# Inverse roots of four group norms at once: GpSimd's power function in place of Newton steps on VectorE

## The chip, the cores and the metric

The kernel runs on one core of one Trainium2 chip. The core has five engines that run side by side, each with an instruction queue of its own that it works through in order: TensorE (PE in the profile; its weight loads are PEld), VectorE (DVE), ScalarE (ACT), GpSimd (POOL) and SyncE (SP), which here only issues DMAs. An instruction that needs another engine's result waits on a semaphore, and everything behind it in its queue waits too. The metric is the device time of one execution in microseconds (us), lower is better.

## The reference

A residual block of a diffusion network on two images of 512 channels and 64 x 64 pixels: group norm with four groups, SiLU, a 3 x 3 convolution, an embedding added per channel, again group norm, SiLU and convolution, and the input added at the end.

```python
def gn(z, gamma, beta):
    zr = z.reshape(B, G, (C // G) * H * W)          # G = 4, eps = 1e-5
    mu = zr.mean(-1).reshape(B, G, 1)
    var = ((zr - mu) ** 2).mean(-1).reshape(B, G, 1)
    zn = ((zr - mu) / jnp.sqrt(var + eps)).reshape(B, C, H, W)
    return zn * gamma.reshape(1, C, 1, 1) + beta.reshape(1, C, 1, 1)
h = conv3(_silu(gn(x, g1, be1)), w1)
emb = _silu(t_emb) @ w_emb
h = h + emb.reshape(B, C, 1, 1)
h = conv3(_silu(gn(h, g2, be2)), w2)
return x + h
```

A group is 128 channels, so it is one channel tile: 128 partitions, one channel each.

## The kernel before

**Tiling.** The work is cut into eight chunks, numbered 0 to 7: layer, then image, then upper or lower half of the image. Each chunk has four channel tiles as input and four as output. For an input tile the kernel loads the half image (`load_a`), applies group norm and SiLU in one ScalarE instruction with a scale and a bias per partition (`silu`, an ACTIVATE of 128x2112 at L371), and turns the rows into planes for a convolution by transform: ScalarE or VectorE makes a scaled copy (the `k` copies, 128x2145), and VectorE adds and subtracts planes (`rows_a`, `rows_b`; L348). For an output tile, `unit` runs the matmuls of all planes (L401), ScalarE evicts PSUM with scales (L371), and VectorE adds the pieces together (names ending in S, A, s, d, y; L348). In the first layer the result goes to `h_scr` in DRAM; in the second it is accumulated by DMA onto the input that has been copied to the output before. The weights are transformed too (`prep_w1`, `nest_w1`, and `prep_w2` with ScalarE copies of 128x384 and VectorE additions of 128x768).

**Group norm.** `gn_chain` (L452) turns sums per partition into the scale S and the bias B that `silu` uses. A matmul with -1/128 averages over the partitions and spreads the result, VectorE copies it out of PSUM (L469), forms the square of the mean minus the mean of squares (L474 and L475, the negative variance), takes the inverse root, and computes S (L492) and B (L497, L498). It comes in two sizes. For the first layer's first image it runs four times with one group each (n = 1, before 31 us); there the inverse root is a GpSimd instruction, a power with exponent -0.5 (L479). For the other three cases it handles four groups at once (n = 4, 128x4 values):

- `st1`: layer 1, image 1. In the trace VectorE works on it from 105.6 to 111.7 us, in chunk 1; the reader is the SiLU of chunk 2 at 111.71 us.
- `gn2_0`: layer 2, image 0. From 170.1 to 204.4 us, in chunk 2; the reader is the SiLU of chunk 4.
- `gn2_1`: layer 2, image 1. From 275.8 to 319.6 us, in chunks 4 and 5; the reader is the SiLU of chunk 6 at 319.87 us. `gn2` adds two instructions behind the chain (L1078, L1079) for the embedding.

In these three the inverse root is made on VectorE: one step that clamps and halves (L482), a first guess from the bits of the number (L485), and three rounds of Newton's method with three instructions each (L488, L489, L490).

**Order.** The function first lists all operations with their reads and writes (`pl.op`), and then issues them in an order written out by hand: the string `ORDER` (L168) has two characters per operation, its number in base 64. `emit` (L97) walks the string. Each engine thus has a fixed sequence, and the instructions of a chain stand wherever the string puts them: in `st1` and `gn2_1` mostly side by side, in `gn2_0` spread between other VectorE work. GpSimd's queue holds, besides small memsets, the DMAs that accumulate (`sw=True`, L386): pieces of a unit's output onto its rows (`oa`), and from chunk 4 on the results onto the output.

**Names of single operations** that the prediction uses: `u10A`, a 128x1024 addition of VectorE for output tile 0 of chunk 1, which reads two evictions; `u10s`, the next addition there, which reads all four.

Of the kernel before, what the change touches and what calls it, by code (L numbers as in the profile page):

```python
# [11 lines left out]
ALU = mybir.AluOpType  # L12
# [103 lines left out]
def _idx(off, dims):  # L116
# [16 lines left out]
EPS = 1e-5  # L133
# [32 lines left out]


ORDER = (  # L168
    "0R0M000O0N2g0P0T0S0Q0p010U020304050607080o0V1J0n1G0e0m1H0k0t0f0l1I0q0s0r0g0u1L1K1M0v0w0h0x1N0y1O0X1P2Z1Q0z0-250Y"
    "0_2W0i0j1R160Z1a1k3P1S0b1T1l101m190W22121n3X1o2C111U2D1d0a1p2p090A0B0C0D0E0F2F0G0H0I0J0K0L1q132E1r1V141s2G2H1t4t"  # L170
    "1C1u3R2I1W152h2J1v2K1w172L1X2M1x3S181D0d1A1F1B2N3Q1Y1y2O1Z1z1b1-2P4Y1E1c1_1e2s1f4g3U202Q21282S233Y2R2429262T271g"
    "2r2c2U2v2V3T2X1h2d2B2Y0c2a2j2b1i2k2A2y2l1j2z3t2i2m2e2-2o4b2u2q2_2f303n2n313k4a323Z333a3u2t4Z343v3b353c364h2x3738"
    "3d2w393e3C3A3f3m3w3q3B3x453D3g5c3F463h4i3E474d3W5U4k484j493V3i4A4c3G4B4l4C3H3y3K4m4F3p3z3I4G3J6Y3j4H3l4n4I3o4J5W"
    "4f4u4x4K3L4L5X5d4M3r3M51424o3-523_4r4O535V4p544e3s554z564D6Q4-4N574E584s4w6l5B5e5C4q6Z5D5g406m5E415F5Y6n5G5h5H85"
    "5I6S5i5f5p4y435k4v5q865r4P6R5s875u5j5v4Q4T4_5wBK4RBL5x503N4S5y5Z4U5z5-445m4V5l5_5J6T995K625A6a63595n64BM5L3O655o"
    "676c685M5P5a696b5N6d6A5OBO6B666eBa9A6C5t7u6f6V6D5Q6E6o4W6g5R6U6p6h6q8y9B6r6kBN6j6t616u6vBSBPBc6w6xBQ606y6zAD6-6F"
    "73Bb6iBT6G746WBR5b6XAE4X75AF5S76BH786H79777A7B6I6L7C7D7EBeBU7F7J6JBIBW6K7KDI6s6M7LDQBd7cBVBg7M6N6_7d70Bf7N7eBJDR"
    "7G7OBh7f725T7gBY7PBX7Q7hBZ7i7j887k7H7l7m897nDJ7R7o718A7p7S7q7IDT8B7rDS7s7T8DDK8E8F7tDU7v8G8HDM8IEr8JDW8KDY8P7U8Q"
    "DV7V7w8R7WDF7X8S7y8L8U7x8T8V8W8X8z7z8Y8Z8aDGA08b7-8f7Y8g8M808h6O7Z8C7_8iDa8N8j8d818n8kDHDL8-8l8cDO8m8_9C8oDN909D"
    "A1DZDP829E919F8OB49H836P9I9J9K9L929M8e9NDX9O9T847b8p9UEs939VDc9W94Ez9Y8q9Z9a9b978s9c9d9e8r9f989j8t959kEt8u9G9l9P"  # L180
    "9mDbEv8v9QA29nF5Eu9S7a9oB5De9pDdA39qA4AG9hE-96AH9XA59gAI9RD29rA6AJ9i9sALA8AMAKAN8wAO9tAPAQA7AR9xASAX9uATAUAYA99w"
    "AZExE_B6Aa9vEwAcF0AdB8EyD3AeAfABAgAhAiAjAn9yF6AoDfAAAk9zApB9AlAqB78xArBAEbACAsAVBCAtAvBBAuAWBiAwBD9-BjF7AmD4BkBG"
    "AxBlBFBnBoA_BpAyBqAbBrBsD6A-BtBuByD5AzBzB-BwB_B0BvC4BmC5C0D7B1BxC6F9C19_C7EoGWBEC9CACdF1CBCCCeEpCDGOCED8F8CFCgEq"
    "CGC8CJChDACKCLCHCMF3CPCNF2CQCID9F4B3CRFBCiDBCSG8FADgC2GYDhDCGQGXFCCTDiCfC3EcCjDEDjGPDDDlDmDnDoCODpDqDtDrDsGSEdDw"
    "CkCUDxDyClGLDzE2GaDuCmCVE3HuGRCnGeGME4CXCoEeGZE5CYCWCpEfE7G9E8E9CqGNEAEBCrEgECEDEECZEHHhEIEJD_EKD-ENGUDvCaCsEODk"
    "EhB2GcEFEPGTE6EiEQGfHwEjFDGgCtGbEGFEGVCuELEkFFE1GAFGCvE0GdFICwEnFJFKGiFLFMEREMFNI0FOFPFRFTHiHyFUFVFWESI8FbElHvFc"
    "CxGCGhFdETFYFeEmEVFgEWFhEUFiGDFjFSFkFlFHGjFmFnEXFQFqFrI2FsFtHxFwGEFXEYCyGkFxFoGBI1FfFyGlJJFZFpFzI4FuCbGFGmCcCzH-"
    "GnC-HzGoGGGpIAFaI9IGF-GIGrGsJKGtI3GKGuGvGHG-GwGzGxGyFvHjH0JLH1H_H2H3I5H8F_EZH9I6H5KaG_HAG0H4D0HBHlIHG2I7G3HDGJHE"
    "HFEaHGHHC_HmHIHJHKG1HNHnHOG4HPHQIBHTHCHkG5HUGqH7KcHVIIKbHoHRHWD1HpIJIOHMH6HXIPHqNZHLIQHtJMHsIRNYITHSIUIVIWIXIKIY"
    "IZHYIaIeIdIfICIgHcIhHZImIcIDIbInHbHaIMIoIjIEIiIpISILIFHrIrJNIsHdItIuG6IvIwIxIyIkHeI_I-J0JPJ1INIqJ2J5IlIzJQJ6J3JO"  # L190
# [23 lines left out]
    "dQdRdScrexdTd8dqdldrdsdndtdIdudidvdmdVdwdxeydkdzdJdjd-d_d9dUe0e1e2dyc6e3e4dLe8e9dXe5eAeBdKeCeDdYeEeFeHdWdaeIeJeK"
    "dZdbeLeMdceNeOeReSeTeUdeeGeVe7eWeXeYePe6edeeefezegeaf0eheiddeZejgCeQekdff5elf6f7emf8gDf9ecfAe-fBfCf2fEfDebfFfGf1"
    "fHh6e_fIfJeofKfLfPenfMfQfRepfSfTfUesfVereqfWfYfZetfafbfcfdfeffevfXfieufjfkfNewflfgfmfOfnfofpfufhfrfvfwfqfxfyfzf-"
    "fsf_g3gEg1gFgGg4g0gHgIgJg7gKg6g5gLftgNgMgOg8gPgQgRgSgTg2gUgYgVgZg9gagbgAgcgdgWgBgegfghgXgggigjgkglgmgngogrgpgsgq"
    "gtgug_gwh0gxh3h2h1gyh5gzh4g-h7gvh8h9hChAhDhB"
)

@with_exitstack
def kernel(
# [115 lines left out]
    def F(c, n=1, parts=P):  # L338
        return R(fs[0:parts, c:c + n], ("F", np.arange(c, c + n)), n)
# [109 lines left out]
    def small(fn, r, w, name, cost=0.125):  # L449
        pl.op("DVE", cost, fn, regs(*r), regs(*w), name)  # L450

    def gn_chain(layer, b, ct, mes, name, SB=7, slack=2.5, n=1, half=False):  # L452
# [20 lines left out]
        else:  # L473
            small(lambda: V.tensor_mul(out=N.ap, in0=T0.ap, in1=T0.ap), [T0], [N], name)  # L474
            small(lambda: V.tensor_add(out=N.ap, in0=N.ap, in1=T1.ap), [N, T1], [N], name)  # L475
        if n == 1:
            small(lambda: V.tensor_scalar(out=N.ap, in0=N.ap, scalar1=-1.0, scalar2=EPS, op0=ALU.mult, op1=ALU.max),  # L477
                  [N], [N], name)
            pl.op("POOL", 0.85, lambda: nc.gpsimd.tensor_tensor(  # L479
                out=F(rs, n).ap, in0=N.ap, in1=F(NEGH, n).ap, op=ALU.pow), regs(N), regs(F(rs, n)), name)  # L480
        else:
            small(lambda: V.tensor_scalar(out=N.ap, in0=N.ap, scalar1=-EPS, scalar2=0.5, op0=ALU.min, op1=ALU.mult),  # L482
                  [N], [N], name)
            y, u = F(rs, n), F(Fc(n), n)
            small(lambda: V.tensor_scalar(out=y.ap.bitcast(I32), in0=N.ap.bitcast(I32), scalar1=-0.5,  # L485
                  scalar2=float(0x5F3759DF - (2 ** 30 + 2 ** 22)), op0=ALU.mult, op1=ALU.add), [N], [y], name)
            for _ in range(3):
                small(lambda: V.tensor_mul(out=u.ap, in0=y.ap, in1=y.ap), [y], [u], name)  # L488
                small(lambda: V.tensor_mul(out=u.ap, in0=u.ap, in1=N.ap), [u, N], [u], name)  # L489
                small(lambda: V.scalar_tensor_tensor(out=y.ap, in0=u.ap, scalar=1.5, in1=y.ap, op0=ALU.add, op1=ALU.mult),  # L490
                      [u, y], [y], name)
        small(lambda: V.tensor_mul(out=S.ap, in0=F(rs, n).ap, in1=F(g, n).ap), [F(rs, n)], [S], name)  # L492
        if n == 1:
            small(lambda: V.scalar_tensor_tensor(  # L494
# [896 lines left out]
```

## Time and profile before

| what | value |
|---|---|
| three runs | 459.97, 460.64 and 460.56 us; median 460.56 us |
| profiled execution, first to last instruction (span) | 459.7 us; the page gives no other total for it |
| TensorE, VectorE, ScalarE, GpSimd busy | 448.6, 436.9, 401.8, 58.1 us |
| granted TensorE clock, mean | 0.995 |
| GpSimd powers (L437, L479) | 567 ns once; 911, 548, 934 and 933 ns |
| VectorE's Newton instructions (L485, L488 to L490) | 30, 148 to 165 ns each |
| GpSimd's DMA issues (L386) | 41, mean 1207 and 1244 ns; waits before them up to 22.3 us |

How to read it: the span is cut into busy time per engine. A line of the profile names the source line and the engine, what is written and read, its shape and count, and then busy time and mean, or, in a timeline, start, length, and in brackets the idle time just before it and what ended that. Successive instructions of VectorE and ScalarE overlap in the drawing by some 0.08 us, and matmuls by more, so that what an instruction costs in time is the distance from its start to the next start. Two facts of the trace help with orientation: TensorE works with almost no gap, and VectorE and ScalarE are each over 85% busy, so a wait in one place is often only the other side of a wait in another.

### The profile page before, as it was taken

The numbers are of one execution on the slowest core, as the hardware profiler recorded it, in microseconds if no ns is written. First come the engines' busy times: TensorE is split into PE (matmuls) and PEld (weight loads), VectorE is DVE, ScalarE is ACT, GpSimd is POOL, SyncE is SP. The second block draws the span as 40 slices with busy tenths as digits, with TensorE's granted clock in tenths as the row PEclk, the third lists the DMA queues.
The fourth block names the chain that finished last, engine by engine and source line by source line (L and its number), as shares of the span: only waits on it lengthen the run. The fifth ranks groups of instructions, "written<-read, shape, count | busy, mean of one in ns | idle before, by whom it ended". The sixth has DMA issues, their size and how long they took to land. (4 is left out here: it accounts for less than half of the span.)

```text
span 459.7 us, 8124 instructions
## 1 busy us (share of the span) xinstructions
PE 448.6 (98%) x2904; PEld 282.8 (62%) x2904; DVE 436.9 (95%) x811; ACT 401.8 (87%) x611; POOL 58.1 (13%) x82
## 2 busy tenths in 40 slices
PE   8999999999999999999999999999999999999995
PEld 4754334455555566566665666676666666787882
DVE  2899999999999999999999999999899999999995
ACT  5689999999989999999999999868989869757662
POOL 2110010111111101111000001212121223111220
PEclk9899999999999999999999999999999999999999
DMA  8963561587666468577877947798796989676674
GB/s 321 399 210 109 170 192 47 144 255 223 165 177 202 126 188 233 150 237 217 269 223 234 363 163 229 192 224 222 172 244 156 280 221 260 157 186 122 133 141 93
DMA packets 43176, 92.49 MB, mean 201 GB/s; under 512 B 6400, under 2 KB 18048, under 8 KB 43136
## 3 DMA queue, kind: packets, MB, share of 16 engines
q1 hardware_dynamic: 32208, 77.60, 50.1%
q0 software_dynamic: 10640, 14.38, 20.2%
q8 instruction: 22, 0.36, 0.3%
q14 instruction: 18, 0.15, 0.1%
q10 hardware_dynamic: 288, 0.01, 0.0%
HBM read 62.25 MB, written 31.32 MB: 204 GB/s over the span
## 5 line engine op out<-in xcount | busy, mean ns | idle before, releaser
L401 PE MATMUL psum<-ar 128*128 128x256 f16 (+2 forms) x2771 | 427.7, 316 | 3.3 <-ACT ar L371 2.0
L348 DVE TENSOR_TENSOR ar<-ar 128x1024 f16<-128x1024 f16 (+7 forms) x630 | 413.2, 719 | 8.2 <-ACT ar L371 5.4
L401 PEld LDWEIGHTS <-ar 128*128 128x128 f16 (+1 forms) x2763 | 268.6, 98 | 158.9 <-issue 6.9
L371 ACT ACTIVATE ar<-ar 128x512 f16<-128x512 f16 (+6 forms) x186 | 187.1, 1041 | 26.5 <-DVE ar L348 25.0
L371 ACT ACTIVATE ar<-psum 128x512 f16<-128x512 f32 (+3 forms) x250 | 158.8, 680 | 18.8 <-PE psum L401 10.3
L371 ACT ACTIVATE ar<-ar,fs 128x2112 f16<-128x2112 bf16 (+1 forms) x32 | 68.8, 2154 | 3.7 <-DVE fs L494 3.7
L386 POOL DMA_DIRECT2D ar<-ar x26 | 30.8, 1207 | 218.4 <-DVE ar L348 192.1
L386 POOL DMA_DIRECT2D out_dram<-ar x15 | 18.7, 1244 | 55.0 <-DMA ar<-ar 40.1
L371 ACT ACTIVATION_READ_ACCUMULATOR ar<-psum 128x1 f32 x104 | 22.6, 217 | 0.0
L352 DVE TENSOR_SCALAR ar<-ar 128x520 f16<-128x520 f16 (+3 forms) x50 | 19.6, 404 | 0.0
L390 POOL MEMSET ar<- 128x65 f16 (+4 forms) x29 | 5.8, 269 | 95.1 <-DVE ar L348 48.9
L401 PEld LDWEIGHTS <-ones_bf 128*128 128x128 bf16 x88 | 9.1, 109 | 7.0 <-issue 2.1
L401 PE MATMUL psum<-ones_bf 128*128 128x512 bf16 x32 | 8.8, 438 | 1.1 <-DVE ones_bf L405 1.1
L401 PE MATMUL psum<-ar,ones_bf 128*128 128x260 bf16 x56 | 8.0, 296 | 0.0
L371 ACT ACTIVATION_READ_ACCUMULATOR ar<-ar 128x1 f32 x36 | 7.2, 201 | 0.0
L401 PEld LDWEIGHTS psum<-fs,ones_neg 128*128 128x128 f32 x36 | 4.6, 191 | 2.6 <-issue 1.6
L401 PE MATMUL psum<-fs,ones_neg 128*128 128x1 f32 (+3 forms) x36 | 4.5, 243 | 1.5 <-DVE fs L1130 1.3
L1125 DVE BATCH_NORM_STATS2 fs<-ar 128x6 f32<-128x512 bf16 x4 | 2.5, 681 | 3.7 <-DMA ar<-in_x_dram 3.7
L479 POOL TENSOR_TENSOR fs<-fs 128x1 f32<-128x1 f32 x4 | 3.3, 832 | 19.6 <-DVE fs L477 19.5
L438 DVE CAST fs<-gparm 128x16 f32<-128x16 bf16 x1 | 0.2, 175 | 3.0 <-DMA gparm<-in_params_dram 3.0
L439 ACT ACTIVATE s_sb<-tparm 128x18 bf16<-128x18 bf16 x1 | 0.2, 218 | 3.1 <-DMA tparm<-in_t_emb_dram 3.1
L401 PE MATMUL psum<-ar,s_sb 128*2 128x512 bf16 x9 | 2.7, 377 | 0.0
(54 smaller groups left out, 24.4 us busy)
## 6 DMA issues: line engine op xcount, KB each, us to landing
ar<-in_w_dram SPq DMA_DIRECT2D x36, 384.0 KB, 5.1
ar<-in_x_dram SPq DMA_DIRECT2D x16, 552.5 KB, 4.7
h_scr<-ar SPq DMA_DIRECT2D x16, 520.0 KB, 5.3
ar<-h_scr SPq DMA_DIRECT2D x16, 520.0 KB, 4.7
out_dram<-in_x_dram SPq DMA_DIRECT2D x30, 260.0 KB, 5.8
out_dram<-ar POOLq DMA_DIRECT2D x15, 520.0 KB, 8.0
ar<-in_x_dram SPq DMA_DIRECT2D x13, 520.0 KB, 4.9
u_scr<-ar SPq DMA_DIRECT2D x16, 384.0 KB, 3.8
```

Source lines behind the costliest of these rows:

```text
L348: pl.op("DVE", 0.075 + 0.000521 * out.n, lambda: nc.vector.tensor_tensor(out=out.ap, in0=a.ap, in1=b.ap, op=op), regs(a, b), regs(out), name)
L352: pl.op("DVE", cost or 0.075 + 0.00026 * out.n, lambda: nc.vector.tensor_scalar(out=out.ap, in0=a.ap, scalar1=s, scalar2=None, op0=ALU.mul ...
L371: lambda: nc.scalar.activation(out=out.ap, in_=a.ap, func=func, scale=sc, **kw), regs(*rr), regs(*ww), name)
L386: lambda: eng.dma_start(out=out, in_=in_, **kw), regs(*r), regs(*w), name, lat=3.2 if sw else None, after=after, sw=sw, seq=seq)
L390: pl.op("POOL" if eng == "gpsimd" else "DVE", 0.08 + 0.0005 * out.n, lambda: e.memset(out.ap, v), (), regs(out), name)
L401: nc.tensor.matmul(out.ap, lhsT=lhsT.ap, rhs=rhs.ap, start=st, stop=sp, skip_group_check=True)
L438: nc.vector.tensor_copy(out=fs[:, GB:GB + 4 * CT], in_=gparm[:])
L439: nc.scalar.activation(out=s_sb[:], in_=tparm[:], func=ACT.Silu)
L479: pl.op("POOL", 0.85, lambda: nc.gpsimd.tensor_tensor(out=F(rs, n).ap, in0=N.ap, in1=F(NEGH, n).ap, op=ALU.pow), regs(N), regs(F(rs, n)), ...
L1125: pl.op("DVE", 0.61, lambda: nc.vector.bn_stats(out=q.ap, in_=e.ap), regs(e), regs(q), nm)
```

## The change

For four groups at once, `gn_chain` now does what it does for one group: a VectorE step that negates and clamps to eps, and one GpSimd power with exponent -0.5 over 128x4 values. The guess and the nine Newton instructions go. Three chains have it, so 30 VectorE instructions are dropped and three GpSimd instructions are added.

```diff
-        if n == 1:
-            small(lambda: V.tensor_scalar(out=N.ap, in0=N.ap, scalar1=-1.0, scalar2=EPS, op0=ALU.mult, op1=ALU.max),
-                  [N], [N], name)
-            pl.op("POOL", 0.85, lambda: nc.gpsimd.tensor_tensor(
-                out=F(rs, n).ap, in0=N.ap, in1=F(NEGH, n).ap, op=ALU.pow), regs(N), regs(F(rs, n)), name)
-        else:
-            small(lambda: V.tensor_scalar(out=N.ap, in0=N.ap, scalar1=-EPS, scalar2=0.5, op0=ALU.min, op1=ALU.mult),
-                  [N], [N], name)
-            y, u = F(rs, n), F(Fc(n), n)
-            small(lambda: V.tensor_scalar(out=y.ap.bitcast(I32), in0=N.ap.bitcast(I32), scalar1=-0.5,
-                  scalar2=float(0x5F3759DF - (2 ** 30 + 2 ** 22)), op0=ALU.mult, op1=ALU.add), [N], [y], name)
-            for _ in range(3):
-                small(lambda: V.tensor_mul(out=u.ap, in0=y.ap, in1=y.ap), [y], [u], name)
-                small(lambda: V.tensor_mul(out=u.ap, in0=u.ap, in1=N.ap), [u, N], [u], name)
-                small(lambda: V.scalar_tensor_tensor(out=y.ap, in0=u.ap, scalar=1.5, in1=y.ap, op0=ALU.add, op1=ALU.mult),
-                      [u, y], [y], name)
+        small(lambda: V.tensor_scalar(out=N.ap, in0=N.ap, scalar1=-1.0, scalar2=EPS, op0=ALU.mult, op1=ALU.max),
+              [N], [N], name)
+        pl.op("POOL", 0.85, lambda: nc.gpsimd.tensor_tensor(
+            out=F(rs, n).ap, in0=N.ap, in1=F(NEGH, n).ap, op=ALU.pow), regs(N), regs(F(rs, n)), name)
```

The string `ORDER` is rewritten too, since the operations behind a chain get smaller numbers. Read back into operations, its sequence is the old one: without the 30 dropped operations, and with the three powers put in, every other operation stands in the same place on every engine. The power of `st1` stands in GpSimd's queue between the DMA issues of 105.52 and 119.19 us of the old trace, that of `gn2_0` between those of 158.22 and 176.30 us, and that of `gn2_1` between those of 312.46 and 316.81 us. On VectorE, L492 keeps its place: in `st1` behind `u10A`, in `gn2_0` where it was at 191.97 us, in `gn2_1` behind the 128x1024 addition that was at 318.02 us.

More of the change, by code (lines that the diff above doesn't have):

```diff
@@ L174 @@
[L174 to L178, printed above, removed]
@@ L214 @@
[L214 to L218, printed above, removed]
+    "0R0M000O0N2g0P0T0S0Q0p010U020304050607080o0V1J0n1G0e0m1H0k0t0f0l1I0q0s0r0g0u1L1K1M0v0w0h0x1N0y1O0X1P2Z1Q0z0-250Y0_2W0i0j"
@@ new lines @@
+    "1R160Z1a1k3P1S0b1T1l101m190W22121n3X1o2C111U2D1d0a1p2p090A0B0C0D0E0F2F0G0H0I0J0K0L1q132E1r1V141s2G2H1t4t1C1u3R2I1W152h2J"
+    "1v2K1w172L1X2M1x3S181D0d1A1F1B2N3Q1Y1y2O1Z1z1b1-2P4Y1E1c1_1e2s1f4g3U202Q21282S233Y2R2429262T271g2r2c2U2v2V3T2X1h2d2B2Y0c"
+    "2a2j2b1i2k2A2y2l1j2z3t2i2m2e2-2o4b2u2q2_2f303n2n313k4a323Z333a3u2t4Z343v3b353c364h2x37383d2w393e3C3A3f3m3w3q3B3x453D3g5c"
+    "3F463h4i3E474d3W5U4k484j493V3i4A4c3G4B4l4C3H3y3K4m4F3p3z3I4G3J6Y3j4H3l4n4I3o4J5W4f4u4x4K3L4L5X5d4M3r3M51424o3-523_4r4O53"
@@ new lines @@
+    "5V4p544e3s554z564D6Q4-4N574E584s4w6l5B5e5C4q6Z5D5g406m5E415F5Y6n5G5h5H7y5I6S5i5f5p4y435k4v5q7z5r4P6R5s7-5u5j5v4Q4T4_5wBB"
+    "4RBC5x503N4S5y5Z4U5z5-445m4V5l5_5J6T905K625A6a63595n64BD5L3O655o676c685M5P5a696b5N6d6A5OBF6B666eBR916C5t7l6f6V6D5Q6E6o4W"
+    "6g5R6U6p6h6q8p926r6kBE6j6t616u6vBJBGBT6w6xBH606y6zA46-6F73BS6iBK6G746WBI5b6XA54X75A65S76B8786H79777A7B6I6L7C7D7EBVBL7F7J"
+    "6JB9BN6K7KD06s6M7LD8BU7cBMBX7M6N6_7d70BW7N7eBAD97G7OBY7f725T7gBP7PBO7Q7hBQ7_7H80D17R71817S7IDB827iDA7j7T84D285867kDC7m87"
@@ L219 @@
+    "fmgDgEgGg6gFgHgIgJgKgLgMgNgQgOgRgPgSgTgagVgbgWgegdgcgXgggYgfgZgigUgjgkgnglgogm"
 )
```

76 lines of the change are left out of this document (36 added, 40 removed).

## The prediction

> **What bounds the kernel now.** I read the busy times first, then TensorE's timeline for the places where it stands still, and last the timelines of VectorE, ScalarE and GpSimd around the three chains that the change touches.
>
> ```profile
> PE 448.6 (98%) x2904; PEld 282.8 (62%) x2904; DVE 436.9 (95%) x811; ACT 401.8 (87%) x611; POOL 58.1 (13%) x82
> ```
>
> Three engines are nearly full, so the share alone doesn't say who decides. TensorE's timeline does (start, length, what, and in brackets the idle time before it with who ended it):
>
> ```profile
> 104.67 49.45 PE L401 MATMUL psum<-ar 128*128 128x512 f16 x274
> 154.82 14.61 PE L401 MATMUL psum<-ar 128*128 128x256 f16 x95 [0.70 <-DVE ar L348]
> ...
> 169.63 98.88 PE L401 MATMUL psum<-ar 128*128 128x256 f16 x630
> 269.57 5.45 PE L401 MATMUL psum<-ar 128*128 128x256 f16 x36 [1.05 <-ACT ar L371]
> ...
> 307.28 5.31 PE L401 MATMUL psum<-ar 128*128 128x256 f16 x34 [0.21 <-ACT ar L371]
> 312.77 33.89 PE L401 MATMUL psum<-ar 128*128 128x256 f16 x246 [0.18 <-DVE ar L348]
> 347.02 67.62 PE L401 MATMUL psum<-ar 128*128 128x512 f16 x488 [0.36 <-ACT ar L371]
> 414.97 39.49 PE L401 MATMUL psum<-ar 128*128 128x256 f16 x328 [0.33 <-ACT ar L371]
> ```
>
> The reader should see blocks of 34 to 99 us without a hole. TensorE is the bound; after the first chain the others hold it up in six places for 0.70 + 1.05 + 0.21 + 0.18 + 0.36 + 0.33 = 2.8 us. A drawn matmul overlaps the next by some 0.16 us, so the six cost about 2.8 + 6 x 0.16 = 3.8 us. Work taken from VectorE shortens the run only if its lead survives up to one of them.
>
> **What is removed.** Per chain ten of eleven VectorE instructions (L485 and three rounds of L488 to L490), 0.16 us each in the rows, 30 x 0.16 = 4.8 us busy. In time it is less, because a small instruction beside an independent one overlaps it. From start to next start: chain st1, 107.97 to 110.05 without the 0.33 us of the addition at 109.44, is 1.75 us. Chain gn2_0, where each lies between long additions, is 10 x 0.073 = 0.73 us (172.95 to 173.02, and so on). Chain gn2_1 is 0.07 + 0.18 + 0.11 + 0.12 + 0.87 + 0.19 = 1.54 us. Together 4.0 us of VectorE. The first step (L482) only changes constants: 0.
>
> **st1: what is late next.** VectorE around the chain:
>
> ```profile
> 107.04 1.02 DVE L348 TENSOR_TENSOR ar<-ar 128x768 f16<-128x768 f16 x2
> 107.97 0.16 DVE L485 TENSOR_SCALAR fs<-fs 128x4 int32<-128x4 int32 x1
> ...
> 109.44 0.42 DVE L348 TENSOR_TENSOR ar<-ar 128x512 f16<-128x512 f16 x1
> 109.77 0.16 DVE L489 TENSOR_TENSOR fs<-fs 128x4 f32<-128x4 f32 x1
> 109.97 0.17 DVE L490 SCALAR_TENSOR_TENSOR fs<-fs 128x4 f32<-128x4 f32 x1
> 110.05 0.68 DVE L348 TENSOR_TENSOR ar<-ar 128x1024 f16<-128x1024 f16 x1
> 110.65 0.15 DVE L492 TENSOR_TENSOR fs<-fs 128x4 f32<-128x4 f32 x1
> ```
>
> and ScalarE in the same time:
>
> ```profile
> 108.80 0.61 ACT L371 ACTIVATE ar<-psum 128x512 f16<-128x512 f32 x1
> ...
> 110.42 1.38 ACT L371 ACTIVATE ar<-ar 128x384 bf16<-128x384 bf16 x3
> 111.71 2.15 ACT L371 ACTIVATE ar<-ar,fs 128x2112 f16<-128x2112 bf16 x1
> ```
>
> With the ten gone, the 512-wide addition starts at 107.97 and ends its slot at 108.30. The 1024-wide addition behind it (u10A) reads the eviction that ScalarE runs from 108.80 to 109.41, so VectorE stands still for 1.1 us and starts it at about 109.44 instead of 110.05. L492 then starts at about 110.05; u10s waits for the eviction that begins at 109.85 and ends at 110.48, and so starts at 110.5 rather than 110.92. The w2 addition at 111.59 reads the second of the three copies at 110.42, which ends at 111.39: at least 0.03 us of signal (the least I see between these two engines), so it can gain 0.17 us. ScalarE cannot come forward itself: it is full from 105 to 112 (7.00 us of 7.00) with inputs that were ready more than 1 us before, and SiLU of chunk 2 at 111.71 sits directly behind those copies. What VectorE does next on that plane waits for this SiLU (113.86; it starts 0.21 us later). So of 1.75 us, 0.17 us are left. From there to 154 VectorE is without idle time, and where it meets ScalarE, ScalarE had itself waited for it (1.66 us before 130.74). The 0.17 us therefore reaches the hole at 154.82: -0.17 us.
>
> **gn2_0.** 0.73 us of lead, but TensorE has no hole from 154.82 to 268. ScalarE waits 0.77 us for TensorE before 209.39, runs without a gap from there to 214.76, and VectorE's first row addition of chunk 4 begins 0.03 us after that. TensorE's clock thus sets both back before the hole at 269.57: 0.
>
> **gn2_1.** 1.54 us of lead in front of VectorE's next idle time:
>
> ```profile
> 318.48 1.51 ACT L371 ACTIVATE ar<-psum 128x1024 f16<-128x1024 f32 x2
> 319.87 2.15 ACT L371 ACTIVATE ar<-ar,fs 128x2112 f16<-128x2112 f16 x1
> 321.91 1.94 ACT L371 ACTIVATE ar<-psum 128x1024 f16<-128x1024 f32 x2
> 323.72 2.01 ACT L371 ACTIVATE ar<-ar 128x2145 f16<-128x2145 f16 x1
> ```
> ```profile
> 323.88 3.33 DVE L348 TENSOR_TENSOR ar<-ar 128x2048 f16<-128x2048 f16 x4 [1.65 <-ACT ar L371]
> ```
>
> The eviction at 318.48 starts 0.04 us after its matmul; behind it ScalarE runs without a gap through the SiLU that reads this chain's scale (ready at 319.59, used at 319.87) to 325.73. The idle 1.65 us becomes about 3.2 us: 0.
>
> **What is added: three powers of 128x4 on GpSimd.** The trace has them only with one column:
>
> ```profile
> L479 POOL TENSOR_TENSOR fs<-fs 128x1 f32<-128x1 f32 x4 | 3.3, 832 | 19.6 <-DVE fs L477 19.5
> 24.94 0.93 POOL L479 TENSOR_TENSOR fs<-fs 128x1 f32<-128x1 f32 x1 [9.41 <-DVE fs L477]
> ```
>
> Bounds: 0.55 us (the second of a pair, at 14.64; nothing makes four columns cheaper than one) and 4 x 0.93 = 3.7 us. I take 1.0 us: the row after a pause (0.93) is what all three will be, and other GpSimd rows grow little with columns (a memset takes 0.09 us for one, 0.55 us for 544). GpSimd's queue is in order. For st1 the DMA issue of 105.52 is over at 106.72 and the next comes at 119.19; for gn2_0 it is free from 159.4 to 176.30. For gn2_1 the issue of 312.46 lasts until 313.67, which delays the power by 0.4 us, and the next comes at 316.81. No DMA is pushed back at 1.0 us; at 3.7 us only that last issue is, to 317.4.
>
> Behind the power's reader, L492, waits all of VectorE. st1: the power starts 0.09 us after L482 (as at 24.94), at 107.22, and ends at 108.2; L492 is due at 110.05, so 1.8 us are to spare. At 3.7 us it ends at 110.9, L492 is 0.35 us later than before, and SiLU at 111.71 and everything up to 154.82 with it: +0.35 us. gn2_0: L492 was at 191.97, 18 us to spare. gn2_1: it ends at 314.7, L492 is due at 317.3, and the SiLU bears 319.05: covered even at 3.7 us. So 0 here, with +0.35 us as far end.
>
> While GpSimd computed at 24.94 to 25.87, VectorE's two 1040-wide additions took 0.70 us each, their mean over all 197. The Trainium skill (SBUF — State Buffer, on the shared port pair) says that a VectorE instruction with two SBUF inputs and a GpSimd instruction that reads SBUF lock each other out; by that rule each power would hold VectorE for up to 0.93 us, and 4.0 us of VectorE would shrink to 1.2 us. This trace shows no such hold on VectorE's side.
>
> **Sum.** -0.17 (st1) + 0 + 0 + 0 (powers) = -0.17 us. The profiled span is 459.7 us, and the sum gives 459.5 us. The page has no separate total for that execution; the median of the runs is 460.56 us, 0.9 us outside the span, and I carry that over: 460.4 us.
>
> **Rivals.**
> Faster: the lead does reach the holes, because ScalarE is not as fixed as I read it (its order stays, but it could start earlier where an input comes earlier). Then the hole at 154.82 closes (0.70 + 0.16), as do those at 269.57 and later, each once: up to 3.1 us, as long as 1.75, 0.73 and 1.54 us cover them (0.86 + 0.73 + 1.54), 457.4 us. For it: three of the six waits end on VectorE or just behind it. Against: the three pins at 111.4, 209.4 and 318.5, each ended by an engine that VectorE doesn't drive there. Chance 0.14.
> Slower: the power is late at st1, after 80 us in which GpSimd issued only DMAs. It decides from 3.4 us on (107.22 to L492's old 110.65); beyond that each us is a us at 154.82. At the far end by rows it is 460.9 us, still within the noise; 5 us would be 462.2 us. For it: the same power took 0.55 us right after another and 0.93 us after a pause, so a pause costs. Against: the first one of the run took 0.57 us. Chance 0.13 for over 0.2%, and 0.04 more for what an earlier VectorE may make its DMAs collide with.
> The Trainium skill (GPSIMD Engine Reference, Instruction dispatch) gives the first call of a freshly loaded GpSimd kernel about 6 us; were the power's code displaced by the DMA work, st1 would be some 3.5 us late, an estimate, near 464 us. No row here shows such a load.
>
> **Numbers.** No change within 0.2% (0.9 us, about what a measurement of this kernel can tell): 0.69, with its own range of 459.7 to 461.1 us. Faster 0.14, slower 0.17. The range 459.0 to 461.8 us leaves out most of the faster rival (0.10) and the worse half of the slower (0.08).
>
> **What would show it.** The changed profile should have VectorE idle for about 1 us before a 1024-wide addition near 109.4, waiting for ScalarE; 3.2 us instead of 1.65 us idle near 324; VectorE busy for 432 us; TensorE's holes near 154 and 269 still there, within 0.2 us; three GpSimd powers of 128x4 near 1.0 us, and no VectorE wait on GpSimd. I am wrong if L492 waits for GpSimd, or if the hole near 154 is gone.

## The result and the profile after

The changed kernel takes 468.31 us (median of 4 runs, 467.76 to 469.03) against 460.26 us of the kernel before on the same chip: ratio 1.018, 95% interval 1.0164 to 1.0197. It is 8 us slower, where 460.4 us was predicted. Its profiled execution has a span of 467.3 us (469.03 us in all), 7.6 us more than the 459.7 us before.

Busy times and the group of the powers, from the page of the changed kernel. Line numbers are now 4 lower up to the function of the norm (L344 is VectorE's plane additions, L367 ScalarE, L382 the DMA issues, L397 the matmuls), and L474 is the power:

```profile
PE 450.2 (96%) x2904; PEld 283.1 (61%) x2904; DVE 434.2 (93%) x781; ACT 401.7 (86%) x611; POOL 80.2 (17%) x85
...
L474 POOL TENSOR_TENSOR fs<-fs 128x1 f32<-128x1 f32 (+1 forms) x7 | 25.7, 3674 | 32.8 <-DVE fs L472 32.7
```

VectorE has 30 instructions and 2.7 us of work less. GpSimd has 3 instructions and 22.1 us more. The mean of 3674 ns mixes shapes, so it takes the timeline to see that one power carries nearly all of it. First the place in the kernel before (start, length, what, idle time before it), then the same stretch of the changed kernel on GpSimd, ScalarE, TensorE and VectorE:

```profile
176.30 1.21 POOL L386 DMA_DIRECT2D ar<-ar  x1 [16.86 <-DVE ar L348]
```
```profile
171.40 18.37 POOL L474 TENSOR_TENSOR fs<-fs 128x4 f32<-128x4 f32 x1 [12.88 <-DVE fs L472]
189.74 2.47 POOL L382 DMA_DIRECT2D ar<-ar  x2
...
193.61 0.60 ACT L367 ACTIVATE ar<-psum 128x512 f16<-128x512 f32 x1 [7.44 <-DMA ar<-ar]
...
184.64 3.45 PE L397 MATMUL psum<-ar 128*128 128x512 f16 x27
194.72 5.46 PE L397 MATMUL psum<-ar 128*128 128x512 f16 x16 [6.62 <-ACT ar L367]
...
195.89 1.64 DVE L344 TENSOR_TENSOR ar<-ar 128x768 f16<-128x768 f16 x3 [7.02 <-ACT ar L367]
```

The power of `gn2_0` lasts 18.37 us. Behind it in GpSimd's queue stands the accumulating DMA `u20oa`, which was issued at 176.30 and is now issued at 189.74. Since VectorE runs about 1 us earlier there than in the old trace, it is some 14 us late. ScalarE waits 7.44 us for that DMA, and TensorE (6.62 us) and VectorE (7.02 us) wait for ScalarE. The power's own reader is not what waits.

The table of stretches around it (length, busy time and instructions of TensorE, weight load, VectorE, ScalarE and GpSimd, granted TensorE clock, DMA share, GB/s) shows a second loss:

```profile
188.00:190.00 2.00, 0.09 (x1) 0.00 (x0) 0.87 (x2) 0.00 (x0) 2.00 (x2) 1.00 0.32 111
190.00:192.00 2.00, 0.00 (x0) 0.00 (x0) 0.00 (x0) 0.00 (x0) 2.00 (x3) 0.89 0.59 172
...
194.00:196.00 2.00, 1.28 (x4) 0.44 (x4) 0.11 (x1) 2.00 (x9) 0.00 (x0) 0.50 1.07 318
196.00:198.00 2.00, 2.00 (x6) 0.68 (x5) 2.00 (x6) 2.00 (x8) 0.00 (x0) 0.50 0.05 17
198.00:200.00 2.00, 2.00 (x9) 0.83 (x8) 2.00 (x6) 2.00 (x4) 0.00 (x0) 0.90 0.14 30
```

From 188.9 to 192 us nothing but GpSimd works on the core. The clock drops in the hole and stays at 0.50 until about 198.4 us (0.90 in the last row means half of it for 0.4 of its 2 us), 3.7 us after the matmuls are back.

The account, from the start of the same matmul in both traces (after minus before): -0.22 us up to 150 us; -0.93 us behind the hole near 154, which is gone; +5.86 us at the matmul that was at 188.85, so the new hole is worth 6.8 us; +7.60 us two microseconds of the old trace later, 1.7 us of half clock; from there constant to the end, +7.6 us.

In the other two chains VectorE did what was forecast, though their powers took 2.07 and 1.95 us where 1.0 us was expected. In `st1` VectorE waits for ScalarE's eviction, and behind `gn2_1` its next idle time grows from 1.65 us:

```profile
108.67 0.69 DVE L344 TENSOR_TENSOR ar<-ar 128x1024 f16<-128x1024 f16 x1 [1.05 <-ACT ar L367]
...
331.49 1.96 DVE L344 TENSOR_TENSOR ar<-ar 128x2048 f16<-128x2048 f16 x2 [2.78 <-ACT ar L367]
```

The question for the experiments is thus why one power takes 18 us where two others take 2, and whether that alone is the loss.

### The profile page after: what moved, and what is told of

The parts are those of the page before. It is cut to its first block, busy times and chain, and to the rows that moved or that the text cites. A ratio compares the mean times of both kernels' runs of the same rounds, so it can differ in the third digit from the quotient of the medians.

```text
span 467.3 us, 8098 instructions
## 1 busy us (share of the span) xinstructions
PE 450.2 (96%) x2904; PEld 283.1 (61%) x2904; DVE 434.2 (93%) x781; ACT 401.7 (86%) x611; POOL 80.2 (17%) x85
## 5 line engine op out<-in xcount | busy, mean ns | idle before, releaser
L397 PE MATMUL psum<-ar 128*128 128x256 f16 (+2 forms) x2771 | 429.7, 317 | 9.2 <-ACT ar L367 8.6
L344 DVE TENSOR_TENSOR ar<-ar 128x1024 f16<-128x1024 f16 (+7 forms) x630 | 412.8, 721 | 19.1 <-ACT ar L367 16.0
L397 PEld LDWEIGHTS <-ar 128*128 128x128 f16 (+1 forms) x2763 | 269.1, 98 | 166.5 <-issue 15.5
L367 ACT ACTIVATE ar<-ar 128x512 f16<-128x512 f16 (+6 forms) x186 | 187.2, 1044 | 24.5 <-DVE ar L344 23.8
L367 ACT ACTIVATE ar<-psum 128x512 f16<-128x512 f32 (+3 forms) x250 | 159.4, 682 | 28.7 <-PE psum L397 12.8
L367 ACT ACTIVATE ar<-ar,fs 128x2112 f16<-128x2112 bf16 (+1 forms) x32 | 69.0, 2159 | 3.7 <-DVE fs L478 3.7
L382 POOL DMA_DIRECT2D ar<-ar x26 | 30.9, 1228 | 182.5 <-DVE ar L344 156.8
L474 POOL TENSOR_TENSOR fs<-fs 128x1 f32<-128x1 f32 (+1 forms) x7 | 25.7, 3674 | 32.8 <-DVE fs L472 32.7
L382 POOL DMA_DIRECT2D out_dram<-ar x15 | 18.7, 1246 | 57.3 <-DMA ar<-ar 40.5
L367 ACT ACTIVATION_READ_ACCUMULATOR ar<-psum 128x1 f32 x104 | 22.9, 220 | 0.0
L397 PEld LDWEIGHTS <-ones_bf 128*128 128x128 bf16 x88 | 9.0, 107 | 6.7 <-issue 1.8
L397 PE MATMUL psum<-ones_bf 128*128 128x512 bf16 x32 | 8.6, 430 | 1.1 <-DVE ones_bf L401 1.1
L397 PE MATMUL psum<-ar,ones_bf 128*128 128x260 bf16 x56 | 7.9, 292 | 0.0
L367 ACT ACTIVATION_READ_ACCUMULATOR ar<-ar 128x1 f32 x36 | 7.3, 202 | 0.0
L397 PEld LDWEIGHTS psum<-fs,ones_neg 128*128 128x128 f32 x36 | 4.6, 191 | 2.6 <-issue 1.6
L397 PE MATMUL psum<-fs,ones_neg 128*128 128x1 f32 (+3 forms) x36 | 4.5, 243 | 1.6 <-DVE fs L1114 1.3
L397 PE MATMUL psum<-ar,s_sb 128*2 128x512 bf16 x9 | 2.7, 377 | 0.0
```

What stands on the lines that cost most here:

```text
L344: pl.op("DVE", 0.075 + 0.000521 * out.n, lambda: nc.vector.tensor_tensor(out=out.ap, in0=a.ap, in1=b.ap, op=op), regs(a, b), regs(out), name)
L367: lambda: nc.scalar.activation(out=out.ap, in_=a.ap, func=func, scale=sc, **kw), regs(*rr), regs(*ww), name)
L382: lambda: eng.dma_start(out=out, in_=in_, **kw), regs(*r), regs(*w), name, lat=3.2 if sw else None, after=after, sw=sw, seq=seq)
L397: nc.tensor.matmul(out.ap, lhsT=lhsT.ap, rhs=rhs.ap, start=st, stop=sp, skip_group_check=True)
L474: pl.op("POOL", 0.85, lambda: nc.gpsimd.tensor_tensor(out=F(rs, n).ap, in0=N.ap, in1=F(NEGH, n).ap, op=ALU.pow), regs(N), regs(F(rs, n)), ...
```

## The experiments

The kernel before, on the same chips, ran at 459.57 to 459.97 us (medians); ratios are against these.

### One chain back, and the reader moved

One chain gets its Newton steps back (e1), or the power's reader on VectorE, the product that gives the scale, moves up directly behind the power (e2).

```diff
 e1, against the kernel before
-        if n == 1:
+        if n == 1 or name in ('st1', 'gn2_1'):
 e2, against the changed kernel: only ORDER; VectorE's scale product of gn2_0 stands directly behind the power
```

> The power stays in st1 and gn2_1; gn2_0 goes back to the guess and the Newton steps on VectorE. Theory (the 128x4 power of gn2_0 gets no turn at the memory while VectorE's instructions follow each other without a gap; the DMA behind it is what costs): all of the 8 us goes, 459.5 to 460.8 us, and the two powers left last about 2 us each. Rival 1 (each power costs something, by blocking VectorE or by its wait): 462 to 466 us. Rival 2 (powers on GpSimd after the DMA work are slow wherever they stand): one of the two left lasts over 5 us.

> All three powers as in the change; in gn2_0 only the reader of the power, the product that gives S, is moved forward on VectorE to right behind the 128x512 scaling that starts near 171.8 us, so that VectorE has to stop there until the power is done. Theory (the power is starved by VectorE): the stop is the gap that the power needs; it lasts 1.5 to 1.8 us from its start near 171.4 us, ending about 0.9 us after VectorE stops, VectorE loses about 1 us, and the run is 459.8 to 461.3 us. Rival (the power is slow at this place by itself: its values, or its code displaced by DMA work): it still lasts some 18 us, VectorE now waits for all of it, and the run is over 470 us.

Measured: e1 459.51 us, 0.999 [0.9975, 1.0004]; e2 459.83 us, 1.000 [0.9988, 1.0012]. The whole loss is in `gn2_0`, and two chains on GpSimd gain nothing. In e2 the timeline has

```profile
170.41 1.62 POOL L475 TENSOR_TENSOR fs<-fs 128x4 f32<-128x4 f32 x1 [12.88 <-DVE fs L473]
...
172.06 0.17 DVE L488 TENSOR_TENSOR fs<-fs 128x4 f32<-128x4 f32 x1 [0.94 <-POOL fs L475]
```

VectorE now stops for the power, and the power takes 1.62 us. So its 18 us are not its work: it had been waiting for VectorE to stop. The same is in the changed kernel's trace. VectorE's rows there show no idle time from the start of the power at 171.40 to 188.87:

```profile
171.20 0.72 DVE L344 TENSOR_TENSOR ar<-ar 128x1040 f16<-128x1040 f16 x1
171.81 0.30 DVE L348 TENSOR_SCALAR ar<-ar 128x512 f16<-128x512 f16 x1
172.01 3.26 DVE L344 TENSOR_TENSOR ar<-ar 128x1040 f16<-128x1040 f16 x5
175.17 0.31 DVE L348 TENSOR_SCALAR ar<-ar 128x520 f16<-128x520 f16 x1
175.38 9.79 DVE L344 TENSOR_TENSOR ar<-ar 128x768 f16<-128x768 f16 x17
185.06 0.30 DVE L348 TENSOR_SCALAR ar<-ar 128x512 f16<-128x512 f16 x1
185.26 2.32 DVE L344 TENSOR_TENSOR ar<-ar 128x1040 f16<-128x1040 f16 x3
187.47 0.32 DVE L348 TENSOR_SCALAR ar<-ar 128x520 f16<-128x520 f16 x1
187.68 1.19 DVE L344 TENSOR_TENSOR ar<-ar 128x768 f16<-128x768 f16 x2
```

The power ends 0.90 us after the gap at 188.87 begins. That gap is itself a wait for ScalarE, which waits for the late DMA. In `st1` and `gn2_1` too the power ends 0.90 and 0.87 us after a gap begins (at 107.62 and 321.99).

### Four columns one by one, and the power behind the DMA

In e3 `gn2_0` has four powers of 128x1 in place of one of 128x4. In e4 only GpSimd's order changes: the power stands behind the issue of `u20oa`, its reader stays where it was.

```diff
 e3
-            pl.op("POOL", 0.85, lambda: nc.gpsimd.tensor_tensor(
-                out=F(rs, n).ap, in0=N.ap, in1=F(NEGH, n).ap, op=ALU.pow), ...
+            for i, w in ([(i, 1) for i in range(n)] if name == "gn2_0" else [(0, n)]):
+                pl.op("POOL", 0.85, lambda i=i, w=w: nc.gpsimd.tensor_tensor(
+                    out=F(rs + i, w).ap, in0=F(nv + i, w).ap, in1=F(NEGH, w).ap, op=ALU.pow), ...
 e4, GpSimd's queue in ORDER
-    power of gn2_0, issue of u20oa
+    issue of u20oa, power of gn2_0
```

> The power of gn2_0 is split into four of 128x1, one behind the other; everything else as in the change. If four columns are what needs a gap in VectorE's stream (the powers of 128x1 at 24.9 and 27.1 us lasted 0.93 us with VectorE busy beside them): four times 0.55 to 0.95 us, done by 175.5 us, before the DMA issue at 176 us, and the run is 459.5 to 461 us. If any power is starved here: the first of them lasts some 18 us like the one of 128x4 and the run is 467 to 470 us.

> The power of gn2_0 is moved in GpSimd's queue to behind the DMA issue that it held up (the accumulation of output tile 0 of chunk 2, at about 176 us); its reader stays at its old place, near 191 us. Theory (the power is starved, and what costs is the DMA behind it, not the power): it is again long, some 13 to 15 us, until VectorE stops at the reader, and then ends 0.9 us later; the next DMA issue, due near 189 us, is late by about 3 us, and VectorE by about 1 us: 460 to 463 us. Rival (the length of the power itself costs, or it is slow by itself): 466 us or more.

Measured: e3 469.31 us, 1.019 [1.0174, 1.0213]; e4 459.78 us, 1.0001 [0.9989, 1.0013]. In e3 the first power, of one column, takes 17.89 us, and the next three 0.54 us each, while VectorE stands still: the wait doesn't come from the number of columns. In e4:

```profile
173.95 1.21 POOL L382 DMA_DIRECT2D ar<-ar  x1 [16.65 <-DVE ar L344]
174.71 15.40 POOL L475 TENSOR_TENSOR fs<-fs 128x4 f32<-128x4 f32 x1
190.07 1.22 POOL L382 DMA_DIRECT2D ar<-ar  x1
...
190.14 0.16 DVE L488 TENSOR_TENSOR fs<-fs 128x4 f32<-128x4 f32 x1 [0.94 <-POOL fs L475]
```

The power still waits 15.4 us, its reader holds VectorE up for 0.94 us, the next DMA is issued at 190.07, 2 us later than in e2 (188.06), and the kernel is as fast as before, a little below the 460 to 463 us expected. So a power of 15 us by itself costs nothing, and neither do 2 us of delay for this next DMA; what costs is the long delay of `u20oa`.

### What lets GpSimd in

Four kernels vary what GpSimd does in `gn2_0` and what VectorE has there. e5: the kernel before with an idle product on GpSimd at the power's place. f2: the same with an idle power. f1: the changed kernel with a product for the power. e6 and f3: the changed kernel with idle sums on VectorE, which have one input: two right behind the power's start, or one later.

```diff
 e5 and f2, against the kernel before (f2: op=ALU.pow)
+            if name == "gn2_0":
+                q = F(Fc(n), n)
+                pl.op("POOL", 0.85, lambda: nc.gpsimd.tensor_tensor(
+                    out=q.ap, in0=N.ap, in1=F(NEGH, n).ap, op=ALU.mult), regs(N), regs(q), name)
 f1, against the changed kernel
+            fn = ALU.mult if name == "gn2_0" else ALU.pow
 e6 (twice) and f3 (once, placed later in ORDER), against the changed kernel
+                small(lambda z=z: V.reduce_sum(out=z.ap, in_=fs[:, 0:16].unsqueeze(1).unsqueeze(1)
+                    .to_broadcast([P, 4, 8, 16]), axis=AX.XY), [], [z], name)
```

> The kernel before, with its Newton steps everywhere, and one more GpSimd instruction: at the place of gn2_0's power a plain product of the same 128x4 values into unused columns, which nobody reads. Theory (any GpSimd instruction that reads SBUF is starved there, and the DMA behind it costs): the product lasts 15 to 19 us, until VectorE stops, and the run is 467 to 470 us though VectorE waits for no result of GpSimd. Rival 1 (the power function is what is slow): the product lasts under 2 us, and the run is 459.5 to 460.7 us. Rival 2 (what costs is that VectorE needs the result): 460 to 461 us. Besides, since st1 is as before here: if the hole of TensorE near 154 us (0.70 us) is there again, its closing in the changed kernel is st1's doing; if it is closed, it was a difference between runs.

> The kernel before, with its Newton steps, plus one power of 128x4 on GpSimd at gn2_0's place that reads the same variances and that nobody reads (the idle product there took 0.79 us and cost nothing). Theory 'the function', strict form (a power gets no turn as long as two-input instructions follow each other): the Newton steps' small two-input instructions don't help, but the one-input ones (the first step's integer shift at 171.1, the clamp-like steps after it) do; the power ends about 0.9 us after one of them begins, under 4 us in all, the DMA leaves on time, 459.3 to 460.5 us. If the removed Newton steps had nothing to do with it: the power lasts to 188 or later and the kernel with Newton is slow too, 467 to 470 us.

> The changed kernel with one word changed: the instruction on GpSimd at gn2_0 multiplies instead of raising to a power (so the scale of that norm is not the reference's; the instructions of all other engines, their order and their number are those of the changed kernel). The idle product beside the Newton steps took 0.79 us, so the question is whether the function or VectorE's stream behind it makes the 18 us. Theory 'the stream': any GpSimd instruction that reads SBUF is shut out by VectorE's additions from 171.4 on; the product ends at 188 to 190 us like the power, its DMA leaves at 188 or later, 467 to 470 us. Theory 'the function': only the power needs more than the turns that these additions leave; the product ends within 2 us, the DMA behind it leaves near 174 to 176, 459.3 to 460.3 us.

> The changed kernel; in gn2_0 VectorE gets two more instructions right behind the 128x512 scaling near 171.8 us: sums over 512 constants, with one SBUF input each and about 0.6 us long, whose results nobody reads. VectorE has no gap then, but some 1.2 us in which it reads one tensor at single rate. Theory A (only instructions with two SBUF inputs, or in a fast mode that reads through both ports, shut GpSimd out): the power lasts 1.4 to 2.2 us and the run is 460 to 461.5 us. Theory B (any VectorE instruction shuts it out, so that only a gap helps): the power lasts some 18 us and the run is 467 to 471 us.

> The changed kernel plus one VectorE sum over 512 constants (one SBUF input, about 0.67 us, nobody reads it) placed two or three microseconds behind the start of gn2_0's power, between two-input additions. Theory 'a waiting power goes at the first one-input stretch': it ends 0.9 us after the two-input addition before the sum is over, so after 3 to 5 us in place of 18, the DMA leaves near its old time, 459.3 to 460.5 us. Rival 'it is settled at the start': the two sums helped because they lay within a microsecond of the power's start; a later one doesn't, 467 to 470 us.

| kernel | time, us | ratio | GpSimd's instruction in `gn2_0`, us |
|---|---|---|---|
| e5 product, Newton kept | 459.50 | 0.9998 [0.9988, 1.0007] | 0.79 |
| f2 power, Newton kept | 459.60 | 0.9992 [0.9981, 1.0003] | 1.62 |
| f1 product, no Newton | 467.23 | 1.016 [1.0139, 1.0179] | 17.53 |
| e6 power, two sums at once | 460.08 | 1.0007 [0.9995, 1.002] | 1.62 |
| f3 power, one sum later | 459.75 | 0.9998 [0.9988, 1.0007] | 3.18 |

After e5 it looked as if only a power had to wait; the 467 to 470 us forecast there for a product did not come. f1 refutes that: without the Newton steps the product waits 17.53 us.

```profile
170.54 17.53 POOL L476 TENSOR_TENSOR fs<-fs 128x4 f32<-128x4 f32 x1 [12.88 <-DVE fs L473]
188.01 2.44 POOL L382 DMA_DIRECT2D ar<-ar  x2
...
194.38 1.64 DVE L344 TENSOR_TENSOR ar<-ar 128x768 f16<-128x768 f16 x3 [6.37 <-ACT ar L367]
```

So the function is not the cause, but what VectorE does meanwhile. In f2 the first Newton instruction (L486: one input, four elements) starts at 170.97:

```profile
170.35 1.62 POOL L483 TENSOR_TENSOR fs<-fs 128x4 f32<-128x4 f32 x1 [12.88 <-DVE fs L479]
...
170.76 0.30 DVE L349 TENSOR_SCALAR ar<-ar 128x512 f16<-128x512 f16 x1
170.97 0.18 DVE L486 TENSOR_SCALAR fs<-fs 128x4 int32<-128x4 int32 x1
```

The wide scaling ahead of it is over at 171.07, and the power ends 0.91 us after that. In f3 it is the sum that ends the wait:

```profile
171.44 3.18 POOL L475 TENSOR_TENSOR fs<-fs 128x4 f32<-128x4 f32 x1 [12.88 <-DVE fs L473]
...
172.05 1.67 DVE L344 TENSOR_TENSOR ar<-ar 128x1040 f16<-128x1040 f16 x3
173.61 0.70 DVE L479 TENSOR_REDUCE fs<-fs 128x4 f32<-128x512 f32 x1
```

The last addition before the sum ends at 173.72, and the power 0.90 us later, at 174.62: the same 0.90 us as after a gap.

### Where else it waits

Three kernels put idle instructions on constants behind the DMA issues of layer 1 in the kernel before (p1: product, copy, power of one column, fill; p2: copy, fill, power of four columns, product of one column; p3: two powers). m1 puts a product behind each of GpSimd's 37 DMA issues from there to the end. m2 does so from `u20oa` on, but without Newton: it is e2 plus the products.

```diff
+                q = F(Fc(n), n)
+                for _ in range(37):        # one behind each DMA issue, by ORDER
+                    pl.op("POOL", 0.85, lambda q=q: nc.gpsimd.tensor_tensor(
+                        out=q.ap, in0=F(EPSC, n).ap, in1=F(NEGH, n).ap, op=ALU.mult), [], regs(q), name)
```

> The kernel before with four GpSimd instructions more, on constants, into unused columns that nobody reads, each behind one of the DMA issues of chunk 1 (near 120.4, 135.3, 148.6 and 159.4 us), where VectorE works without gaps over 0.03 us: a product of 128x4 (two inputs), a copy of 128x4 (one input), a power of 128x1, and a memset of 128x4 (no input). Theory: all but the memset are starved until VectorE's next gap or stop; the memset takes under 0.4 us. Rival (only two-input GpSimd instructions are starved): the copy is short too. How long a gap of VectorE must be is read from where each ends.

> As the other kernel with four extra instructions, in another order: a copy of 128x4 near 120.4 us, a memset of 128x4 near 135.3 us, a power of 128x4 near 148.6 us and a product of 128x1 near 159.4 us. Theory: the kind decides and not the place, so the memset is short at its new place and the three that read SBUF are starved until VectorE's next gap or stop. Rival (the place decides): the memset is long here or the copy short in one place and long in the other.

> The kernel before plus two powers of 128x4 on constants that nobody reads, on GpSimd behind the DMA issues of 117.3 and 156.3 us, where a product, a copy or a fill took at most 1.2 us. Theory 'the function': the first, which has two-input additions around it except for one 2145-wide scaling at 119.3, lasts until that scaling or, if a scaling doesn't count, until VectorE's next gap near 134.9, and then pushes the DMA issue of 132.2 back; the second ends 0.9 us after the sum over 56 columns at 158.3 begins. Theory 'something particular to gn2_0's place': both last about 1.6 us, as the one at 146.3 did.

Measured: p1 459.39, p2 459.64, p3 460.03 us, each one run. No probe took over 1.7 us. In p3 the first stood behind the issue of 132.7 us, not of 117.3 as its expectation says; it took 1.57 us with additions of two inputs around it and no gap before its end. That spoke for "something particular to gn2_0's place".

> The kernel before plus an idle product of 128x4 constants on GpSimd behind each of its DMA issues from u10oa (117 us) to the end, 37 of them, to see where in VectorE's stream a GpSimd instruction that reads SBUF has to wait, and how long. Probes so far behind the issues of 117, 132, 146 and 156 us ended within 1.7 us of their start although two-input additions followed each other there. Theory 'the place' (what VectorE runs in a stretch decides, whatever the operands): those four are short again, the one behind u20oa (174.3) is long, up to 14 us, unless one of the last Newton steps falls behind its start, and others after long unbroken stretches of two-input additions are long too; a product that lasts until the next DMA issue delays that one. Theory 'the operands' (only an instruction that reads what VectorE has just computed waits): all 37 end within 1.5 us.

> The kernel with three powers and the reader of gn2_0's power directly behind it (459.8 us, power 1.6 us), plus the same idle product of constants behind each of GpSimd's DMA issues from u20oa (175.3) to the end. In the kernel with the power behind u20oa that power waited 15.4 us in the same stretch, with VectorE's additions in the same order. Theory 'the place': the product behind u20oa lasts until about 188 to 190 us as well; a DMA is due at 187.6, so about 0 to 2 us of delay and 459.5 to 462 us. Theory 'the operands': it ends within 1.5 us of its start; 459.5 to 460.3 us.

Measured: m1 464.08, m2 466.78 us (one run each, beside 459.59). The same product on the same constants behind the same DMA, with Newton steps (m1) and without (m2):

```profile
175.16 1.85 POOL L484 TENSOR_TENSOR fs<-fs 128x4 f32<-128x4 f32 x1
...
174.69 2.24 DVE L345 TENSOR_TENSOR ar<-ar 128x768 f16<-128x768 f16 x4
176.85 0.17 DVE L490 TENSOR_TENSOR fs<-fs 128x4 f32<-128x4 f32 x1
```
```profile
176.37 14.99 POOL L481 TENSOR_TENSOR fs<-fs 128x4 f32<-128x4 f32 x1
191.31 1.19 POOL L383 DMA_DIRECT2D ar<-ar  x1
...
175.81 9.77 DVE L345 TENSOR_TENSOR ar<-ar 128x768 f16<-128x768 f16 x17
...
191.21 0.17 DVE L499 TENSOR_TENSOR fs<-fs 128x4 f32<-128x4 f32 x1
```

In m1 it ends at 177.00, with a Newton product of four elements (176.85 to 177.01). In m2 that instruction is gone, and it ends at 191.37, with the next four-element instruction there is. This settles it against "the operands": constants wait as long as fresh variances. It is the place, and the Newton steps had been, by their small size, what opened VectorE's stream.

The wait in m2 is the one that was expected, but the time is not (459.5 to 462 us). The wait behind `u20oa` isn't what costs there: at 211.6 us of e2's trace TensorE is only 0.6 us behind e2. The rest, 6.1 us, is lost behind 294 us, 2.9 us of it where the product of chunk 4 waits as in m1 below; what makes up the remainder is not shown.

m1 also shows that a stretch can hold GpSimd up with no power in the kernel at all, in chunk 4:

```profile
282.42 11.50 POOL L484 TENSOR_TENSOR fs<-fs 128x4 f32<-128x4 f32 x1
293.87 0.86 POOL L383 DMA_DIRECT2D ar<-ar  x1
...
296.53 2.92 ACT L368 ACTIVATE ar<-psum 128x512 f16<-128x512 f32 x4 [4.05 <-DMA ar<-ar]
...
297.18 7.11 PE L398 MATMUL psum<-ar 128*128 128x512 f16 x32 [2.61 <-ACT ar L368]
```

The same chain as in the changed kernel, wait, late DMA, ScalarE, hole in TensorE, makes m1 4.5 us slower: against e5's trace, TensorE's matmuls are 4.4 us later just behind this stretch and 4.3 us later at the end. The shape of the waits in m1 is uneven. The last product apart, 32 of 36 ended within 1.5 us of the end of the issue ahead, mostly 0.03 to 0.07 us after one of VectorE's additions ended. The other four waited 3.2, 5.4, 10.4 and 11.2 us through 5 to 21 ends of VectorE instructions, and ended at a gap of 0.03 or 0.10 us. What decides whether the first handover lets GpSimd in stays open: the same pairs of additions occur on both sides.

No kernel here is measurably faster than the one before. TensorE, busy for 98% of the span, sets its end, and the VectorE time saved doesn't show in the total.

## Why the prediction was wrong

**What failed: "Bounds: 0.55 us ... and 4 x 0.93 = 3.7 us" with "nothing makes four columns cheaper than one".** The far end took the length of a one-column power as work that grows with columns. Columns are not what is long: once VectorE stands still, the power ends 0.43 us later with one column (e3) and 0.90 us later with four, and in e2 it takes 1.62 us in all. The rest, in the 18.37 us some 17.5, is waiting, and no multiple of a row bounds that: it ends when VectorE breaks its stream. So the term that failed is the 0 of the powers, and what was missing in it is a wait for VectorE. The 0.93 us at 24.94 already held some of it: VectorE ran a two-input addition from 24.77 to 25.47, and the power ended 0.40 us after that. The prediction read this as the price of a pause.

**"This trace shows no such hold on VectorE's side."** True, and the wrong side. By the rule of the Trainium skill that the prediction cites (SBUF — State Buffer, on the shared port pair), either engine can lock the other out. I priced VectorE held by GpSimd (4.0 us shrinking to 1.2) and never GpSimd held by VectorE, though VectorE, 95% busy and nearly all of that with two-input additions, is the one that is mostly there first. The length of GpSimd's wait had to be read from VectorE's timeline behind each power: no idle time and nothing but wide additions and a few fp16 scalings for 17 us, once the Newton steps are gone.

**"No DMA is pushed back at 1.0 us"** fell with the duration. The issue of `u20oa` was due 4.0 us after the start of the power (170.35 and 174.34 in f2), so a longer power pushes it back. Not every microsecond of that counts: some 14 us of delay made a hole of 6.62 us in TensorE. The prediction looked at L492 there, "18 us to spare", and that held: in e4 the reader waits 0.94 us, at no cost. The deadline was that of the instruction behind the power in its queue, not that of its reader.

**The slower rival** had the right sign and mechanism (a late power) at the wrong place: `st1`, deciding at 3.4 us, 460.9 to 462.2 us. The power of `st1` took 2.07 us and delayed nothing. No load of code showed: the powers of `st1` and `gn2_1` took 2.07 and 1.95 us, 0.90 and 0.87 us of it behind a gap, after 80 and 130 us without one at work.

**What held.** The removal: VectorE 432 us forecast, 434.2 measured; the instructions that remain are on average 3 ns longer. `st1`: VectorE idle for 1.05 us before the 1024-wide addition (forecast 1.1); the w2 addition behind it comes 0.93 us earlier than before, of which 0.78 us were there at 103 us, before anything removed, so the chain gave 0.15 us (forecast 0.17). `gn2_1`: idle 2.78 us in place of 1.65 (forecast 3.2), and TensorE's next hole behind it, 0.36 us at 347.02 in the old trace, is 0.36 us again: 0. The clue "I am wrong if ... the hole near 154 is gone" was badly chosen. It is gone, but it is gone too in e5, whose `st1` keeps the Newton steps:

```profile
103.37 64.19 PE L398 MATMUL psum<-ar 128*128 128x512 f16 x369
```

In p2, with the Newton steps too, it is 0.25 us. The 0.70 us of the first profile were one execution's, not the kernel's. One reading of the old trace was loose too, though nothing hangs on it: "blocks of 34 to 99 us" are rows of the view, and from hole to hole it is 5.3 to 113.7 us.

The sum by its terms, in the profiled executions: forecast -0.17 (st1) + 0 (gn2_0) + 0 (gn2_1) + 0 (powers). Measured: 0.15 us of lead at `st1`, with no hole left for it to close; nothing gained at `gn2_0` or `gn2_1`; and +6.8 and +1.7 us for the power of `gn2_0` (hole and half clock). Another -0.2 us comes from the first microseconds and -0.7 us from the missing hole near 154, which e5 lacks without the change. That makes the +7.6 us.

## What to carry to other kernels

Before a small operation moves to GpSimd, read VectorE's timeline at its place: it may have to wait until VectorE has a gap, a one-input sum or an instruction of a few elements, and in a stream of wide two-input additions that was up to 18 us. Then look at what stands behind it in GpSimd's queue, DMAs above all, because their deadline counts and not only the reader's. Work that looks removable from a busy engine may be what opens that engine's stream for another: the cheap mends here (the reader directly behind the power, the DMA ahead of it, one idle sum) all bring the time back to 459.8 us, and none below the time before.

## What the runs showed of the hardware that was not expected

- GpSimd instructions that read SBUF (power or product, fresh values or constants) can wait while VectorE runs two-input additions back to back, though at 32 of 36 places in m1 they hardly did. The long ones took 15.4, 17.5, 17.9 and 18.4 us in `gn2_0`, and one in chunk 4 waited 11.2 us. The wait ends 0.06 us (product), 0.43 us (power of one column) or 0.90 us (power of four columns) before the instruction does. A VectorE gap of 0.03 us is enough to end it, as are a one-input sum and a four-element addition. VectorE's fp16 scalings of 512 and 520 elements did not end it in the changed kernel (at 171.81, 175.17, 185.06 and 187.47), though in p2 a power ended 0.90 us after the addition ahead of such a scaling, the first to end behind the DMA issue.
- The Trainium skill (SBUF — State Buffer, "Summary: rules for kernel authors") states the lock of the two engines with the second one fully blocked until the first has finished. The quick cases agree, with GpSimd done 0.03 to 0.07 us after an addition's end. The long ones go beyond it: GpSimd let 15 (in chunk 4 of m1) to 26 (in m2) ends of VectorE instructions pass.
- Issuing a DMA on GpSimd showed no such wait: the issue took 1.21 us in e4, beside additions like those that held the power behind it for 15.4 us. Whether filling memory waits is not shown: the fill in p1 was over 0.12 us after the issue ahead of it, but at a place where a product was short too (p2).
- A hole of 6.6 us cost TensorE 6.8 us of half clock, from about 191.6 to 198.4 us, worth 1.7 us on top. The Trainium skill (TensorE: Matmul & The Clock Gate, "What's actually happening") gives windows of about 3.4 us for going down and up again; the trace agrees: down 3.5 us after the last matmul, up 3.7 us after the next.
